# An S4D convolution with a token MLP: magnitude products moved into the openings of the sets, and the results of rows and columns taken out of PSUM behind the second half of E

## The chip, the cores and the metric

The kernel runs on one core of a Trainium2 chip. The metric is the device time of one execution in microseconds; lower is better.

## The reference, cut to what matters

```python
x = A_u                                                   # (1, 2048, 448)
mod = (silu(c) @ w_mod).reshape(..., 6, 1, -1)            # sa, ca, ga, sb, cb, gb
h = layernorm(x) * (1 + ca) + sa
# S4D: K[d, l] = 2 Re sum_n C[d, n] dt[d] exp((-exp(log_A_real) + i A_imag)[d, n] dt[d] l)
#      y = irfft(rfft(h, 4096) * rfft(K, 4096))[:2048] + h * D_skip        (d: 448, n: 256, l: 2048)
x = x + ga * S4D(h)
h = layernorm(x) * (1 + cb) + sb
x = x + gb * (gelu(h^T @ w1 + b1) @ w2 + b2)^T            # a token MLP, 2048 -> 1792 -> 2048
```

## The kernel before, in words

All of it is float32. The first half of the time makes the S4D convolution, the second half is the token MLP, which the change does not touch. The convolution is a Fourier transform in two stages. The transform of u (the normalised input) is made in **rows** (`u_rows`: 32 of them, each one matmul of 448 columns into PSUM and one VectorE instruction, L595, that adds the mean and multiplies by `mod`; two rows, a *pair*, share a tile `yt` of [128, 2, 448], and a pair's second row issues the DMA of the tile to `yu_d` in DRAM, L597) and then in **columns** (`u_cols`: 16 of them, each 8 matmuls of 448 columns into two PSUM tiles and two VectorE instructions, L631, and a DMA to `us_d`). Row pair p reads `xt[:, p]` and nothing else of `xt`.

The kernel K is generated in 56 *halves* s (16 channels of a group at a time). A half has these parts:

- **exponents and magnitudes** (`st_exponents`, `st_exp`): two Exp on ScalarE (L696) into `mag`;
- **phase** (`st_phase`, L667): eight matmuls on TensorE into the PSUM tiles `xe` and `xg`, of which there are two sets, so the phase of half s+1 writes where the E products of half s-1 have read;
- **sines** (`st_step`): six ScalarE instructions (L729 to L735);
- **G**: two products on GpSimd (L737, L738);
- **m2**, the magnitude product (`st_mag2`): a small product `w` (L712) and a large one (L717, `m`) on GpSimd;
- **E**: four products on VectorE, a first half E1 (L739, L740) that reads xe, and a second half E0 (L742, L743) that reads xg; two of the four read m2;
- **kgen** (`st_kgen`, L764): 64 small matmuls of E and G into `kg`, two halves later.

Every eighth half begins a *set*. `window(s)` first runs Exp for all eight halves of the set, e = 0 to 7 (Exp and Sin need different tables on ScalarE), and puts other work beside it; then the eight *steps* follow, one `st_step` each. Below, "window 8" is the opening of the set of halves 8 to 15, and "step 8" its first step. Ahead of the change the window computes m2 for the first two halves of its set (e < 2), and step s computes m2 of half s+2.

The instruction order of TensorE, ScalarE, VectorE and GpSimd is that of the code. What is not to run at once goes into lists of functions: `dve` for VectorE, `act` for ScalarE. `flush(dve)` is called by `between()`, which stands in `st_step` between E1 and E0; so the results of rows or columns whose matmuls stand behind step s are taken out of PSUM in step s+1, between its E1 and its E0. The rows and columns, `st_s1` (the next stage of K, L802) and the modulation share one pool of three PSUM tiles, `pms`. When `st_s1` has work in a step, `free` is false and the step gets no rows or columns. From half 8 on the order of SyncE, which issues nearly all DMAs, is a scheduler's.

`chain(q)` prepares the parameters of a group of 128 channels in small VectorE instructions, and `split` (L404, L406) cuts each result into two parts on GpSimd (`hl`, two buffers) and stores it to DRAM (`pars`). It runs mostly in the windows: `more(n)` makes n of its steps. Tile `xa` has one buffer; in window 16 ScalarE writes it for q = 3 (L451) when GpSimd's split of the old one is done. Set 32 and later run otherwise (`late_window`), and the change leaves them.

Pool `gp_` has three buffers of E, [128, 2, 16, 64]. Row pairs 2, 3 and 4 borrow E buffers (`yE`) for their `yt`; the other pairs share three buffers of `yt`. `m2p` has three buffers of m2. Weights of the modulation are loaded into `xt` (`wm_load`, L341, at steps 12 to 14 of the code): `xt[:, 0:4]`, then 4:8, then 8:12.

## Time and profile before

| | |
|---|---|
| runs | 663.27, 663.41, 668.56 us; median 663.41 us |
| profiled execution | 663.85 us, span 662.1 us, mean granted TensorE clock 0.984 |
| busy share of the span | PE 92%, DVE 67%, ACT 66%, POOL 41% |
| window 8 and its steps (us of the span) | about 64.7 to 82 and 82 to 114 |
| window 16 and its steps | about 114 to 133 and 133 to 163 |
| window 24 and its steps | about 163 to 178 and 178 to 206 |

PE is TensorE, DVE VectorE, ACT ScalarE, POOL GpSimd, SP SyncE; a row of the timeline gives the start, the duration and the instruction, and in brackets the idle time of its engine just ahead of it, with what ended it. Shares over the whole span mix the convolution with the MLP; the stretches in the table are where the changed code runs.

### The profile page before, as it was taken

Reading aid. Unit: us, or ns where it says so; the run is one execution under the profiler, and the core shown is the slowest. Engines: PE = TensorE matmul, PEld = TensorE weight load, DVE = VectorE, ACT = ScalarE, POOL = GpSimd, SP = SyncE. Lnnn points to the kernel's source line nnn. Section 1 sums busy time; section 2 is a strip of 40 time slices with the busy share of each in tenths; the row PEclk is TensorE's granted clock in tenths of the full one; section 3 lists DMA queues with packets and bytes.
Section 4 is the critical chain, followed back from the end, with each engine's and each line's share of the span. In section 5 each row is a group of like instructions: output and inputs, shape, how many; then the busy total and the mean of one; then the engine's idle time right before and its main releaser. Section 6 shows DMA issues by size and latency. Waiting matters only on the chain.

```text
span 662.1 us, 19161 instructions
## 1 busy us (share of the span) xinstructions
PE 612.3 (92%) x7639; PEld 442.9 (67%) x7639; DVE 443.0 (67%) x853; ACT 439.9 (66%) x828; POOL 269.5 (41%) x351
## 2 busy tenths in 40 slices
PE   1878998999999999999888999999999999999997
PEld 0444555445455565656544577788999999999996
DVE  8989889689894887868655688777422553333331
ACT  5978888899989999999587678885222522222220
POOL 7785597588599788787563000000000000000000
PEclk9998999989999999999999899999999999999999
DMA  6595747598775557576787999946755275555530
GB/s 145 156 219 166 253 143 257 182 248 268 218 247 178 103 166 218 169 215 182 234 274 227 257 247 234 233 112 196 201 160 153 57 209 164 162 160 166 161 106 28
DMA packets 97858, 123.67 MB, mean 187 GB/s; under 512 B 13717, under 2 KB 79801, under 8 KB 97769
## 3 DMA queue, kind: packets, MB, share of 16 engines
q1 hardware_dynamic: 97032, 120.02, 64.2%
q0 software_dynamic: 736, 2.43, 1.5%
q8 instruction: 60, 0.98, 0.7%
q14 instruction: 30, 0.24, 0.1%
HBM read 88.33 MB, written 33.59 MB: 184 GB/s over the span
## 4 chain that ended last, share of the span: by engine, by line
PE 63%; DMA 11%; DVE 9%; ACT 7%; POOL 4%; issue 4%; SPq 3%; ACTq 0%; DVEq 0%; POOLq 0%
PE o L1563 7%; PE o L1565 7%; PE o L1564 7%; PE acc L1400 6%; PE acc L1401 6%; PE acc L1402 6%; PE xe L667 6%; PE kg L764 6%; DMA w<-in_B_w_dram 3%; PE xg L667 3%; DMA xt<-in_A_u_dram 3%; DMA v_d<-vt 3%; PE pu L591 2%; PE vv L895 2%; PE kx L872 2%
## 5 line engine op out<-in xcount | busy, mean ns | idle before, releaser
L218 ACT CAST whi<-w 128x896 fp32r<-128x896 f32 x64 | 59.7, 939 | 138.5 <-PE o L1564 82.7
L227 DVE TENSOR_TENSOR wlo<-w,whi 128x896 fp32r<-128x896 f32 x64 | 68.1, 1086 | 41.4 <-ACT whi L218 35.1
L737 POOL TENSOR_TENSOR G<-mag,gs 128x512 f32<-128x512 f32 x56 | 71.9, 1283 | 36.4 <-ACT gs L733 36.4
L1400 PE MATMUL acc<-h3h,whi 128*128 128x448 f32 x224 | 83.0, 371 | 1.7 <-ACT h3h L1467 0.9
L1401 PE MATMUL acc<-h3l,whi 128*128 128x448 f32 x224 | 81.4, 363 | 0.5 <-DVE h3l L1474 0.3
L1563 PE MATMUL o<-uh,whi 128*128 128x448 f32 x224 | 81.3, 363 | 0.0
L1565 PE MATMUL o<-uh,wlo 128*128 128x448 f32 x224 | 81.2, 362 | 0.0
L1402 PE MATMUL acc<-h3h,wlo 128*128 128x448 f32 x224 | 81.0, 361 | 0.0
L1564 PE MATMUL o<-ul,whi 128*128 128x448 f32 x224 | 80.6, 360 | 0.0
L764 PEld LDWEIGHTS kg<-E,G 128*32 128x32 f32 x3584 | 56.2, 114 | 33.1 <-issue 18.4
L738 POOL TENSOR_TENSOR G<-mag,gs 128x512 f32<-128x512 f32 x56 | 71.9, 1285 | 0.0
L764 PE MATMUL kg<-E,G 128*32 128x64 f32 x3584 | 65.9, 227 | 6.4 <-issue 4.2
L667 PE MATMUL xg<-tab,lph 64*128 64x512 f32 x112 | 62.0, 553 | 6.6 <-DVE E L743 4.3
L1568 DVE TENSOR_TENSOR y<-o,x 128x448 f32<-128x448 f32 x16 | 10.0, 624 | 79.0 <-PE o L1565 79.0
L667 PE MATMUL xe<-tab,lph 64*128 64x512 f32 x112 | 61.9, 553 | 0.3 <-issue 0.2
L717 POOL TENSOR_TENSOR m<-mag,w 128x512 f32<-128x512 f32 x53 | 55.8, 1053 | 4.2
L1400 PEld LDWEIGHTS acc<-h3h,whi 128*128 128x128 f32 x224 | 42.0, 188 | 14.8 <-issue 2.1
L729 ACT ACTIVATE ab<-xe 128x512 f32<-128x512 f32 x56 | 33.9, 604 | 16.3 <-PE xg L667 9.1
L1401 PEld LDWEIGHTS acc<-h3l,whi 128*128 128x128 f32 x224 | 42.0, 187 | 3.8 <-DVE h3l L1474 0.9
L1565 PEld LDWEIGHTS o<-uh,wlo 128*128 128x128 f32 x224 | 42.1, 188 | 3.4
L1402 PEld LDWEIGHTS acc<-h3h,wlo 128*128 128x128 f32 x224 | 42.0, 187 | 3.1
L1564 PEld LDWEIGHTS o<-ul,whi 128*128 128x128 f32 x224 | 41.9, 187 | 3.0
(257 smaller groups left out, 1399.1 us busy)
## 6 DMA issues: line engine op xcount, KB each, us to landing
w<-in_B_w_dram SPq DMA_DIRECT2D x64, 224.0 KB
w<-in_B_w_dram SPq DMA_DIRECT2D x32, 448.0 KB
yi<-yu_d SPq DMA_DIRECT2D x32, 224.0 KB
us_d<-uo SPq DMA_DIRECT2D x16, 448.0 KB
u<-us_d SPq DMA_DIRECT2D x64, 112.0 KB
v_d<-vt SPq DMA_DIRECT2D x32, 224.0 KB
vt<-v_d SPq DMA_DIRECT2D x14, 448.0 KB
yu_d<-yt SPq DMA_DIRECT2D x13, 448.0 KB
```

Source lines behind the costliest of these rows:

```text
L218: self.nc.scalar.copy(hi, w)
L227: eng.tensor_tensor(lo, w, hi.bitcast(F32), ALU.subtract)
L667: T.matmul(out[k], lhs[r], rhs[r], start=start, stop=stop)
L737: G.tensor_tensor(Gt[:, 1], mg_, v32(sg), ALU.mult)
L738: G.tensor_tensor(Gt[:, 0], mg_, v32(cg_), ALU.mult)
L764: T.matmul(kg[32 * q : 32 * q + 32, m], Gt[:, c, d], E[:, c, d], start=h == 0 and c == 0 and m == 0, stop=h == 1 and c == 1, skip_group_ch ...
L1400: nc.tensor.matmul(acc[f], hi[:, fs], h3h[:, r], start=r == 0, stop=False)
L1401: nc.tensor.matmul(acc[f], hi[:, fs], h3l[:, r], start=False, stop=False)
L1402: nc.tensor.matmul(acc[f], lo[:, fs], h3h[:, r], start=False, stop=r == 15)
L1563: nc.tensor.matmul(o, hi[:, ks], uh[kh][:, k], start=kh == 0 and k == 0, stop=False)
L1564: nc.tensor.matmul(o, hi[:, ks], ul[kh][:, k], start=False, stop=False)
L1565: nc.tensor.matmul(o, lo[:, ks], uh[kh][:, k], start=False, stop=kh == 1 and k == 6)
```

## The change: what it does

1. **m2 in the sets.** Windows 8, 16 and 24 compute m2 for the first 4, 5 and 5 halves (`MSET`), where they computed it for 2; the steps compute 4, 3 and 3 where they computed 6 each. For the first two halves of a set m2 goes into an E buffer (`mE`) that the window takes.
2. **Rows by pairs.** Steps 8 to 14 make two rows each (14), where steps 9 to 14 made two or three (15); window 16 makes one more. No row pair borrows an E buffer any more: pairs 3, 4, 6, 8 and 14 use parts of `xt` that have been read (`spare`).
3. **Results at once.** In the steps of sets 8, 16 and 24 the results of rows and columns are taken out of PSUM at the end of the same step, behind E0 (`at_once`), not between E1 and E0 of the next. `more(pace[s])` moves to the end of the step too; where it stood it made no instruction in these sets.

```diff
-        yts, wurs, lent = {}, {}, []
+        yts, wurs = {}, {}
+        spare = {3: 0, 4: 1, 6: 2, 8: 3, 14: 6}
...
-                if pair in (2, 4):
-                    E = gp_.tile([P, 2, GD, NJ], F32, tag="E", name="yE")
...
-                yts[R, gp] = lent[pair - 2] if 2 <= pair < 5 else xp.tile([P, 2, D], F32, tag="yt", name="yt", bufs=3)
+                if pair in spare:
+                    yts[R, gp] = xt[:, 2 * spare[pair] : 2 * spare[pair] + 2]
+                else:
+                    yts[R, gp] = xp.tile([P, 2, D], F32, tag="yt", name="yt", bufs=3)
...
-            if s in (3, 4, 5):
+            if s in rooms:
+                m2 = rooms.pop(s)
+            elif s in (3, 4, 5):
...
+        def at_once(f, it, n):
+            k = len(dve)
+            some(f, it, n)
+            for out in dve[k:]:
+                out()
+            del dve[k:]
...
+            if s in (8, 16, 24):
+                E = gp_.tile([P, 2, GD, NJ], F32, tag="E", name="mE")
+                for k in range(2):
+                    rooms[s + k] = E[:, k].rearrange("p g j -> p (g j)")[:, 0:512].rearrange("p (d i) -> p d i", i=32)
...
-                elif s and (e < 2 or s >= 32):
+                elif s and e < (BATCH if s >= 32 else MSET[s // BATCH]):
                     st_mag2(s + e)
...
+        MSET = [0, 4, 5, 5]
...
-                if s < len(pace):
+                if s < len(pace) and not 8 <= s < 32:
                     more(pace[s])
...
+            if s == 8:
+                at_once(u_rows, rows, 2)
...
-            if s + 2 < 32 and (s + 2) % BATCH > 1 and s + 2 > 5:
+            if s + 2 < 32 and (s + 2) % BATCH >= max(2, MSET[s // BATCH]) and s + 2 > 5:
                 st_mag2(s + 2)
...
-            if 8 <= s < 16 and free:
-                some(u_rows, rows, 2 if s % 2 else 3)
+            if 8 < s < 16 and free:
+                at_once(u_rows, rows, 2)
...
             if 17 <= s < 32 and free:
-                some(u_cols, cols, 1)
+                at_once(u_cols, cols, 1)
+            if 8 <= s < 32 and s % BATCH != BATCH - 1:
+                more(pace[s])
```

VectorE in steps 10 and 11, before (E1 is L739 and L740, E0 is L742 and L743; `yt<-pu` are results of rows):

```order
L739 TENSOR_TENSOR E<-m_1359,xe 128x16x32
L740 SCALAR_TENSOR_TENSOR E<-mag,xe 128x16x32
L595 SCALAR_TENSOR_TENSOR yt<-pu,means,mod_105 128x448 x2
L742 TENSOR_TENSOR E<-mag,xg 128x16x32
L743 TENSOR_TENSOR E<-m_1359,xg 128x16x32
L739 TENSOR_TENSOR E<-m_1402,xe 128x16x32
L740 SCALAR_TENSOR_TENSOR E<-mag,xe 128x16x32
L595 SCALAR_TENSOR_TENSOR yt<-pu,means,mod_105 128x448 x3
L742 TENSOR_TENSOR E<-mag,xg 128x16x32
L743 TENSOR_TENSOR E<-m_1402,xg 128x16x32
```

The same place of the changed kernel (its lines are two further down; `xt<-pu` is a pair that uses a part of `xt`):

```order
L741 TENSOR_TENSOR E<-m_1140,xe 128x16x32
L742 SCALAR_TENSOR_TENSOR E<-mag,xe 128x16x32
L744 TENSOR_TENSOR E<-mag,xg 128x16x32
L745 TENSOR_TENSOR E<-m_1140,xg 128x16x32
L595 SCALAR_TENSOR_TENSOR xt<-pu,means,mod_105 128x448 x2
L741 TENSOR_TENSOR E<-m_1170,xe 128x16x32
L742 SCALAR_TENSOR_TENSOR E<-mag,xe 128x16x32
L744 TENSOR_TENSOR E<-mag,xg 128x16x32
L745 TENSOR_TENSOR E<-m_1170,xg 128x16x32
L595 SCALAR_TENSOR_TENSOR yt<-pu,means,mod_105 128x448 x2
```

The results have moved from between E1 and E0 to behind E0, ahead of the next step's E1, and there are two to a step.

GpSimd in window 16, before (`hl` are the chain's splits, `ks` a small sum for `st_s1`):

```order
L404 CAST hl<-ph 128x256
L784 TENSOR_TENSOR ks<-ks,dsk 128x8
L406 TENSOR_TENSOR hl<-ph,hl 128x256
L404 CAST hl<-p_1199 128x256
L406 TENSOR_TENSOR hl<-p_1199,hl 128x256
L404 CAST hl<-xa 128x256
L406 TENSOR_TENSOR hl<-xa,hl 128x256
```

And in the changed kernel:

```order
L404 CAST hl<-ph 128x256
L712 TENSOR_TENSOR w<-mag 128x16
L719 TENSOR_TENSOR m_2047<-mag,w 128x512
L786 TENSOR_TENSOR ks<-ks,dsk 128x8
L406 TENSOR_TENSOR hl<-ph,hl 128x256
L404 CAST hl<-p_1206 128x256
L712 TENSOR_TENSOR w<-mag 128x16
L719 TENSOR_TENSOR m_2075<-mag,w 128x512
L406 TENSOR_TENSOR hl<-p_1206,hl 128x256
L712 TENSOR_TENSOR w<-mag 128x16
L719 TENSOR_TENSOR m_2094<-mag,w 128x512
L404 CAST hl<-xa 128x256
```

Three pairs `w`, `m` stand ahead of the last split (`hl<-xa`) that stood behind step 16 to 18's G before.

SyncE in the steps of set 8, changed kernel (`yu_d<-xt` stores a pair out of `xt`, `yu_d<-yt` one out of a `yt` buffer; `xt<-in_w_mod_dram` are weights):

```order
L597 DMA yu_d<-xt 128x896
L341 DMA xt<-in_w_mod_dram 112x4x448
L597 DMA yu_d<-yt 128x896
L653 DMA lph_139<-pars_58 32x256
L657 DMA lph_139<-pars_58 64x1x256
L597 DMA yu_d<-yt 128x896
L341 DMA xt<-in_w_mod_dram 112x4x448
```

The first row is pair 8's store; the weights behind it overwrite the part of `xt` that it reads, so they now wait for that store to land, and pair 9's store stands behind them. Before, the weights waited there for matmuls alone.

More of the change, by code (lines that the diff above doesn't have):

```diff
@@ L581, in u_rows @@
                 pair = n // 2
-                if pair in (2, 4):
-                    E = gp_.tile([P, 2, GD, NJ], F32, tag="E", name="yE")
-                    rooms = E.rearrange("p a g j -> p (a g j)")[:, 0 : 4 * D].rearrange("p (h g d) -> p h g d", h=2, g=2)
-                    lent.extend(rooms[:, h] for h in range(2))
-                yts[R, gp] = lent[pair - 2] if 2 <= pair < 5 else xp.tile([P, 2, D], F32, tag="yt", name="yt", bufs=3)
+                if pair in spare:
+                    yts[R, gp] = xt[:, 2 * spare[pair] : 2 * spare[pair] + 2]
+                else:
+                    yts[R, gp] = xp.tile([P, 2, D], F32, tag="yt", name="yt", bufs=3)
             if g == 0 and R < 6:
@@ L639, in u_cols @@
                 u_load(p + 4)
-        mags, m2s, eg, phs = {}, {}, {}, {}
+        mags, m2s, eg, phs, rooms = {}, {}, {}, {}, {}
         v32 = lambda t: t.rearrange("p (d i) -> p d i", i=32)
```

## The prediction

> **What bounds the kernel now.** The page says where the whole time goes: TensorE is busy for 92%, and most of its chain is the MLP, which the change leaves. So I read the three stretches that it touches, each from the first sine of a set to the last.
>
> Busy time of each engine by stretch (us, instructions in brackets):
>
> ```profile
> core 0: us, PE busy (x) PEld busy (x) DVE busy (x) ACT busy (x) POOL busy (x), PEclk, DMA share, GB/s
> 78.90:111.30 32.40, 30.06 (x562) 17.02 (x558) 28.82 (x50) 27.61 (x53) 27.57 (x31) 1.00 0.69 218
> 130.90:160.30 29.40, 28.14 (x515) 14.83 (x516) 26.53 (x47) 27.00 (x54) 25.30 (x28) 0.94 0.92 252
> 174.30:204.40 30.10, 27.95 (x608) 15.58 (x610) 27.80 (x47) 27.11 (x52) 27.06 (x32) 1.00 0.73 232
> ```
>
> No engine has much room: DVE, ACT and POOL are each busy for 86 to 92% there. A step must be looked at singly. Steps 27 and 28 on POOL, then on DVE, then on PE (timeline, start and duration):
>
> ```profile
> 189.74 1.28 POOL L737 TENSOR_TENSOR G<-mag,gs 128x512 f32<-128x512 f32 x1
> ...
> 192.22 0.25 POOL L712 TENSOR_TENSOR w<-mag 128x16 f32<-128x16 f32 x1
> 192.54 1.05 POOL L717 TENSOR_TENSOR m<-mag,w 128x512 f32<-128x512 f32 x1
> 193.55 1.27 POOL L737 TENSOR_TENSOR G<-mag,gs 128x512 f32<-128x512 f32 x1
> ...
> 192.06 0.68 DVE L739 TENSOR_TENSOR E<-m,xe 128x512 f32<-128x512 f32 x1
> ...
> 193.26 1.26 DVE L631 SCALAR_TENSOR_TENSOR uo<-mod,svt,pu 128x448 f32<-128x448 f32 x2
> 194.44 0.68 DVE L742 TENSOR_TENSOR E<-mag,xg 128x512 f32<-128x512 f32 x1
> ...
> 195.64 0.68 DVE L739 TENSOR_TENSOR E<-m,xe 128x512 f32<-128x512 f32 x1
> ...
> 191.31 1.10 PE L764 MATMUL kg<-E,G 128*32 128x64 f32 x64
> ...
> 193.45 1.51 PE L627 MATMUL pu<-yi,s 64*64 64x448 f32 x8
> ```
>
> POOL has no gap and a period of 193.55 - 189.74 = 3.81 us, of which `w` and `m` take 193.55 - 192.22 = 1.33. DVE has none either, with a period of 195.64 - 192.06 = 3.58: four E products at 0.60 and two results (`uo`) at 0.59 from start to start. On PE 193.45 - 191.31 = 2.14 hold kgen (1.03) and the phase (1.1); the columns' matmuls behind them (`pu`) take 1.51, since they wait for a PSUM tile that DVE empties. POOL is the slower one and yet does not set the pace, since kgen needs G two halves later. It does once in the set, in its last step, on ACT:
>
> ```profile
> 202.49 0.60 ACT L733 ACTIVATE gs<-xg 128x512 f32<-128x512 f32 x1 [0.52 <-POOL G L737]
> ```
>
> So in the middle of a set **DVE is the bound**, and POOL's lag is paid once, at 0.52 us. Where else DVE waits is the next question; steps 9 to 15 on DVE:
>
> ```profile
> 85.58 0.69 DVE L739 TENSOR_TENSOR E<-m,xe 128x512 f32<-128x512 f32 x1 [0.58 <-ACT xe L732]
> 89.63 0.69 DVE L739 TENSOR_TENSOR E<-m,xe 128x512 f32<-128x512 f32 x1 [1.24 <-POOL w L712]
> ...
> 104.32 1.27 DVE L595 SCALAR_TENSOR_TENSOR yt<-pu,means,mod 128x448 f32<-128x448 f32 x2 [1.50 <-DMA yu_d<-yt]
> ...
> 114.44 1.28 DVE L808 COPY yk<-y 128x512 f32<-128x512 f32 x2
> ```
>
> and where POOL and DVE begin the set:
>
> ```profile
> 82.54 1.29 POOL L737 TENSOR_TENSOR G<-mag,gs 128x512 f32<-128x512 f32 x1 [5.55 <-ACT gs L733]
> 82.54 0.68 DVE L739 TENSOR_TENSOR E<-m,xe 128x512 f32<-128x512 f32 x1
> ```
>
> **The change, part by part.**
>
> *Set 8: -2.9 us.* E of half 8 starts at 82.54, and the copies behind E of half 15 start at 114.44: 31.9 us. In them lie 32 E products at 0.60 (19.1) and 15 results at 0.595 (8.9), so 28.0 of work and 3.9 of waiting. Afterwards there are 14 results (8.3), so 27.4 of work. Of the waits, 0.58 goes, since the two results of step 8 now fill it. The 1.50 goes as well: it is a store that had not landed when its `yt` buffer was wanted again, and with `spare` the buffers are wanted later (the pair that waits is three pairs after its buffer's last user, and pairs 8 and 14 no longer take one). The 1.24 is named for POOL, but `w` cannot hold E1; ACT was late:
>
> ```profile
> 87.92 0.64 ACT L729 ACTIVATE ab<-xe 128x512 f32<-128x512 f32 x1
> 83.81 1.16 PE L802 MATMUL y<-wc,ks 64*64 64x64 f32 x64
> 84.90 1.26 PE L679 MATMUL kg<-ones 128*128 128x256 bf16 x10
> ```
>
> A new wait takes its place. `y` needs two of the three PSUM tiles of `pms`; with the two rows of step 8 ahead of it on PE, one of its tiles is free only when DVE has taken out the first result, at about 84.9 + 0.6 = 85.5 instead of 83.8. Behind `y` on PE's queue stand the ten warming matmuls and the phase of half 10, so that phase ends at about 85.5 + 1.1 + 1.2 + 1.1 = 88.9, ACT starts half 10 there and not at 87.92, and DVE waits about 1.0 for the rows of step 9, which stand behind that phase. I keep 1.2 of waiting in all: 82.5 + 27.4 + 1.2 = 111.1 and about 0.2 of loose ends, so 111.3 against 114.4 on DVE; ACT's last sine comes about 2.9 earlier. From both ends: 0 (the waits come back elsewhere) to -4.5 (all 3.9 go, and a result).
>
> *Window 8: +0.15.* POOL makes two more pairs `w`, `m` there, 2.7 us; its wait of 5.55 ahead of the first G (above) covers them. But one pair stands ahead of `ks`, which `y` needs:
>
> ```profile
> 73.67 0.21 POOL L784 TENSOR_TENSOR ks<-ks,dsk 128x8 f32<-128x8 f32 x1
> 75.03 1.52 PE L802 MATMUL y<-wc,ks 64*64 64x64 f32 x64
> ```
>
> `ks` ends 1.33 later, at 75.2, and PE takes `y` at 75.03 now. Bounds 0 and 1.33.
>
> *Window 16: +1.4.* Three pairs more, 3 x 1.32 = 3.96, in the middle of the chain's splits. POOL waits there as follows:
>
> ```profile
> 124.06 0.40 POOL L404 CAST hl<-ph 128x256 fp32r<-128x256 f32 x1 [1.22 <-DVE ph L419]
> 125.73 0.40 POOL L404 CAST hl<-p 128x256 fp32r<-128x256 f32 x1 [0.35 <-DVE p L425]
> 129.19 0.40 POOL L404 CAST hl<-xa 128x256 fp32r<-128x256 f32 x1 [2.25 <-DVE xa L445]
> 129.66 0.72 POOL L406 TENSOR_TENSOR hl<-xa,hl 128x256 fp32r<-128x256 f32 x1
> 130.53 0.35 ACT L451 ACTIVATE xa<-A_C_real 128x128 f32<-128x128 f32 x1
> ```
>
> The pairs stand behind the first of these splits, so the idle 0.35 and 2.25 behind them cover 2.60; the remaining 3.96 - 2.60 = 1.36 makes `hl<-xa` end at 131.7 instead of 130.38. L451 on ACT overwrites `xa`, started at 130.53, 0.15 after that end, and has all sines of half 16 behind it on ACT's queue. So what is off the path in POOL's idle time sits on the path at this one place: the set starts 1.2 to 1.4 later, and I take 1.4. Lower end 0. Upper end: DVE's own products with two SBUF operands may be held by POOL's; the same instruction took
>
> ```profile
> 62.13 0.43 DVE L434 TENSOR_TENSOR xa<-xa,A_C_real 128x256 f32<-128x256 f32 x1
> 126.31 0.91 DVE L434 TENSOR_TENSOR xa<-xa,A_C_real 128x256 f32<-128x256 f32 x1
> ```
>
> with POOL idle and with POOL in a split. Three such holds of 0.48 give +1.4 more, so +2.8 for the upper end. The Trainium skill's page "SBUF — State Buffer", section "Who interferes with whom", has a rule for it that speaks against this change: a DVE instruction with two SBUF inputs and a GpSimd one that reads SBUF exclude each other, and the second to come is blocked until the first ends. [...] By the rule each moved `m` could hold a DVE product for its whole 1.05; three of them would make this window 3.2 worse, and the sum +0.5 in place of -2.65.
>
> *Set 16: -0.8.* Here the columns' results now run where DVE waited for ACT.
>
> ```profile
> 137.96 2.17 PE L627 MATMUL pu<-yi,s 64*64 64x448 f32 x8
> 143.14 0.98 PE L627 MATMUL pu<-yi,s 64*64 64x448 f32 x8
> 143.30 0.60 ACT L729 ACTIVATE ab<-xe 128x512 f32<-128x512 f32 x1 [1.27 <-PE xg L667]
> 144.97 0.69 DVE L739 TENSOR_TENSOR E<-m,xe 128x512 f32<-128x512 f32 x1 [0.69 <-POOL w L712]
> 147.36 0.68 DVE L742 TENSOR_TENSOR E<-mag,xg 128x512 f32<-128x512 f32 x1
> ```
>
> The first columns take PE 2.17 us where the next take 0.98 (their data come late), phase 19 follows late, ACT waits, and E1 of half 19 starts at 144.97. Then the results of step 18 went ahead of E0 (147.36). Now they stand ahead of E1, in DVE's waiting time: matmuls done at 143.14 + 0.98 = 144.1, results to 145.3, E1 to 146.5, E0 from 146.5: 0.8 earlier. From there DVE has no gap, before or after, and the gain keeps its size. Bounds 0 and -1.5 (all of DVE's waits in the set's first four steps).
>
> *Set 24: -0.5.* DVE runs without a gap through the first six steps, and E0 of each half ends where it did, since the same results come ahead of it; E1 comes later, which nobody waits for. PE no longer waits for a PSUM tile (1.51 above for columns that take 0.98), but DVE was the bound. What is left is ACT's 0.52 for POOL, which goes, as POOL has three pairs less. In window 24 the three pairs again stand among splits; the last split ends perhaps 0.9 later and so does G of half 24, but kgen of that half stands two steps later, and G of the next halves catches up without its `m`, so I cost it at nothing; if that cover went it would be 0.9.
>
> The eight pairs taken off POOL in the steps, 8 x 1.33 = 10.6, are therefore worth only the 0.5. Sets 32 to 48 keep their code and move as a block.
>
> **Sum:** -2.9 + 0.15 + 1.4 - 0.8 - 0.5 = -2.65, against the profiled execution's 663.85: 661.2. That execution was 0.44 above the median of the runs (663.41), to which the new runs will be compared, so I predict **660.8**, or 0.4% less. About 1% is what can be told from no change here.
>
> **Rivals.**
>
> *POOL is the bound after all* (the change does what its words suggest): every pair saved shortens its step, 663.4 - 10.6 = 652.8. For it: POOL without a gap in all three sets. Against it: DVE without a gap at 3.58 beside POOL's 3.81, and a single wait of ACT for G. Chance 0.03.
>
> *The splits hide the moved pairs:* window 16 costs nothing, since the 0.15 of slack is larger than shown or DVE is earlier; 660.8 - 1.4 - 0.15 = 659.2. For it: POOL is busy for half of each window. Against: the 1.36 above. Chance 0.20.
>
> *SyncE gives set 8's gain back.* The loads of `w_mod` into `xt` now wait in SyncE's order for pair stores to land, with pair 9's store behind; step 14's results want that buffer.
>
> ```profile
> 96.50 7.72 DMA yu_d<-yt
> ```
>
> In the chain of waits a store lands 7.72 us after its issue. Pair 8's results end at about 94.5 and its store lands between 98 and 102 (half of 7.72, and all of it); then pair 9's store takes until 102 to 110. By my count the buffer is wanted at 107.7. At the late end DVE waits 2.3 there and the stores behind add to it, so set 8's 2.9 is gone: 663.7. For it: the DMA share of 0.69 in that stretch. Against: only the ends together are late. Chance 0.15.
>
> *POOL's moved products hold DVE's.* The hold of 0.48 shown above meets the chain's products in windows 16 and 24 six times: 2.9, so 663.7. For it: those two rows. Against: DVE has waits of its own in the windows that would take part of it. The page named above would have each hold last up to 1.05, which makes 6.3 and 667.1. Chance 0.08.
>
> *The results stand in DVE's way* (the other side). `at_once` puts DVE behind matmuls of the same step at 18 places, with the next E1 queued behind the result. From the end of the last E0, PE needs 1.1 for the phase and 0.98 for the columns, DVE gets there after 3.58: slack 1.5. It decides when PE runs more than 1.5 late in each step, as where columns took 2.17 for 0.98 (+1.19) and kgen 1.86 for 1.03 (+0.83):
>
> ```profile
> 140.13 1.86 PE kg L764 x64
> ```
>
> Together 2.02, so 0.5 a step and 9 us over 18 steps without set 16's and 24's gains (1.3): 660.8 + 9 + 1.3 = 671; in half of the steps 666.6. Against it: in the steady part PE has 1.03 + 1.1 + 0.98 = 3.1 of work for 3.58. Chance 0.08, half of that over 1% slower.
>
> **How the numbers follow.** Forecast 0.46 (its own range 659.7 to 662.4, each term within half of its bounds), rivals 0.03, 0.20, 0.15, 0.08 and 0.08. The range from 658.4 (hidden pairs, and all of set 16's waits) to 664.4 (either of the two at 663.7, and window 24's 0.9) leaves out the first and the last rival and some tail. Faster by over 1%: the first rival and a tail of the second, 0.04. Slower by over 1%: 0.04. Within: 0.92.
>
> **What would show it.** Right: DVE from E of half 8 to the copies behind half 15 in about 29 us; L451 in window 16 waiting for POOL's L406 by over 1 us; no ACT wait for G in step 31; POOL with gaps in the sets, without gain from them. Wrong: DVE waits ahead of L595 or L631 for PE in most steps; a DMA wait at step 14; a period below 3.5 us in the middle of a set.

## The result and the profile after

| | before | after |
|---|---|---|
| median of 12 runs each, in turn | 664.22 us (662.07 to 669.44) | 668.85 us (666.13 to 672.97) |
| ratio, 95% interval | | 1.0072 [1.0048, 1.0096] |
| span of the profiled execution, mean granted clock | 662.1 us, 0.984 | 665.5 us, 0.982 |

The changed kernel is 0.7% slower; 660.8 us was forecast, within 658.4 to 664.4. The page's first block, after:

```profile
span 665.5 us, 19164 instructions
PE 609.0 (92%) x7639; PEld 444.0 (67%) x7639; DVE 447.9 (67%) x853; ACT 440.5 (66%) x828; POOL 270.9 (41%) x351
```

Each engine has as many instructions as before, but DVE is busy for 4.9 us more (443.0 before): single DVE instructions have become longer. The loss is read by stage. In the table a window runs from its first Exp (L696) to the second E1 product of its first half (L742 after, L740 before); set 8 runs from there to the last sine of half 15 (L737, L735 before), and set 16 or 24 to the first Exp of the next window. The last column is the start of half 33's first E0 product (L744, L742 before), and behind it all kernels have the same instructions. The labels are those of the experiments below.

| us | window 8 | set 8 | window 16 | set 16 | window 24 | set 24 | half 33 at |
|---|---|---|---|---|---|---|---|
| before | 18.43 | 27.66 | 18.50 | 29.90 | 15.05 | 26.17 | 221.77 |
| after | 19.22 | 28.33 | 20.92 | 28.82 | 16.12 | 25.55 | 225.40 |
| e1_products_only | 21.18 | 27.06 | 19.49 | 30.59 | 15.61 | 25.78 | 225.16 |
| e2_rows_only | 18.67 | 27.22 | 17.54 | 29.88 | 15.21 | 25.78 | 220.71 |
| e3_step8_behind | 19.55 | 28.81 | 20.87 | 28.95 | 16.44 | 25.55 | 226.49 |
| e4_windows_8_only | 20.03 | 26.98 | 17.54 | 29.90 | 15.33 | 25.77 | 221.73 |
| e5_no_rows_in_8 | 20.31 | 25.71 | 24.13 | 29.40 | 16.26 | 25.55 | 227.10 |
| e6_late_pairs | 19.82 | 27.99 | 19.68 | 28.48 | 15.15 | 27.56 | 224.28 |
| e7_memsets | 18.66 | 27.21 | 20.32 | 29.86 | 16.01 | 25.81 | 224.23 |
| e8_products_twice | 19.18 | 26.98 | 19.96 | 29.84 | 15.54 | 26.07 | 224.11 |
| e10_rows_only_9_10 | 19.59 | 26.40 | 18.37 | 29.89 | 14.61 | 26.45 | 220.99 |
| e11_window_8_rows_9_10 | 20.27 | 25.72 | 18.75 | 29.87 | 14.55 | 27.03 | 221.68 |
| e12_third_pair_early | 18.95 | 26.70 | 18.14 | 29.53 | 15.76 | 25.56 | 221.33 |
| e13_rows_9_10_again | 19.33 | 25.69 | 24.37 | 29.15 | 15.91 | 25.56 | 226.71 |
| e14_windows_16_24 | 19.00 | 26.65 | 19.95 | 30.01 | 16.42 | 25.57 | 223.70 |

How far profiles differ without a change of the code is seen in stretches with the same instructions: window 8 with two pairs takes 18.43 to 19.59, and the stretch from half 33 to the end 440.1 to 444.4. A single cell is good to about 1 us; below, the table is used where several rows agree, and the timed ratios for the rest. (The profile of e9_rows_9_10 was taken in a disturbed execution and isn't used; e13_rows_9_10_again is the same kernel.)

**Window 16.** DVE in the changed kernel:

```profile
126.02 0.85 DVE L423 TENSOR_SCALAR u<-ph 128x256 f32<-128x256 f32 x1
126.91 0.99 DVE L425 TENSOR_TENSOR p<-ph,u 128x256 f32<-128x256 f32 x1
...
128.88 1.14 DVE L436 TENSOR_SCALAR A_C_imag<-A_C_imag 128x256 f32<-128x256 f32 x1
130.05 0.84 DVE L438 SCALAR_TENSOR_TENSOR xa<-xa,A_C_imag 128x256 f32<-128x256 f32 x1
...
131.39 1.02 DVE L443 TENSOR_SCALAR u<-xa 128x256 f32<-128x256 f32 x1
132.44 0.43 DVE L445 TENSOR_TENSOR xa<-xa,u 128x256 f32<-128x256 f32 x1
```

POOL at the same time, and ACT behind it:

```profile
125.67 1.05 POOL L719 TENSOR_TENSOR m<-mag,w 128x512 f32<-128x512 f32 x1
...
126.89 0.72 POOL L406 TENSOR_TENSOR hl<-ph,hl 128x256 fp32r<-128x256 f32 x1
128.69 1.18 POOL L719 TENSOR_TENSOR m<-mag,w 128x512 f32<-128x512 f32 x1
129.84 0.77 POOL L406 TENSOR_TENSOR hl<-p,hl 128x256 fp32r<-128x256 f32 x1
131.07 1.19 POOL L719 TENSOR_TENSOR m<-mag,w 128x512 f32<-128x512 f32 x1
132.94 0.40 POOL L404 CAST hl<-xa 128x256 fp32r<-128x256 f32 x1 [0.68 <-DVE xa L445]
...
134.17 0.31 ACT L451 ACTIVATE xa<-A_C_real 128x128 f32<-128x128 f32 x1 [2.33 <-POOL hl L406]
```

The three moved products end at 126.72, 129.87 and 132.26; L423, L436 and L443 of DVE end at 126.87, 130.02 and 132.41, each 0.15 behind one of them. L425 and L438 end in the same way, 0.3 behind the two L406. The stretch from L423's start to L445's end takes 132.87 - 126.02 = 6.85 us. The same on DVE in e2_rows_only, which has two products in this window, as before:

```profile
123.83 0.36 DVE L423 TENSOR_SCALAR u<-ph 128x256 f32<-128x256 f32 x1
124.23 0.43 DVE L425 TENSOR_TENSOR p<-ph,u 128x256 f32<-128x256 f32 x1
...
126.13 0.28 DVE L436 TENSOR_SCALAR A_C_imag<-A_C_imag 128x256 f32<-128x256 f32 x1
126.45 0.43 DVE L438 SCALAR_TENSOR_TENSOR xa<-xa,A_C_imag 128x256 f32<-128x256 f32 x1
...
127.36 0.29 DVE L443 TENSOR_SCALAR u<-xa 128x256 f32<-128x256 f32 x1
127.69 0.43 DVE L445 TENSOR_TENSOR xa<-xa,u 128x256 f32<-128x256 f32 x1
```

It takes 128.12 - 123.83 = 4.29. So of the 3.4 us by which window 16 is longer than in e2_rows_only, 2.56 are held DVE instructions, not a delay in POOL's queue: POOL waits for DVE (0.68 ahead of `hl<-xa`), and not the other way. This does not vary from profile to profile: the stretch takes 6.84 to 6.95 in all seven with the three products among the splits (the changed kernel, e1, e3, e5, e8, e13, e14), 4.28 or 4.29 in the six without (e2, e4, e6, e10, e11, e12), and 4.6 before.

**Set 8.** The waits went and came back. DVE, PE and ACT in the set, after:

```profile
86.81 1.28 DVE L595 SCALAR_TENSOR_TENSOR xt<-pu,means,mod 128x448 f32<-128x448 f32 x2 [1.27 <-PE pu L591]
91.80 1.27 DVE L595 SCALAR_TENSOR_TENSOR yt<-pu,means,mod 128x448 f32<-128x448 f32 x2 [1.33 <-PE pu L591]
87.55 1.15 PE L804 MATMUL y<-wc,ks 64*64 64x64 f32 x62 [0.52 <-DVE xt L595]
85.62 0.60 ACT L731 ACTIVATE ab<-xe 128x512 f32<-128x512 f32 x1 [2.12 <-PE xg L667]
91.10 0.60 ACT L731 ACTIVATE ab<-xe 128x512 f32<-128x512 f32 x1 [1.29 <-PE xg L667]
102.79 0.60 ACT L735 ACTIVATE gs<-xg 128x512 f32<-128x512 f32 x1 [0.27 <-POOL G L739]
107.17 0.60 ACT L735 ACTIVATE gs<-xg 128x512 f32<-128x512 f32 x1 [1.01 <-POOL G L739]
110.98 0.60 ACT L735 ACTIVATE gs<-xg 128x512 f32<-128x512 f32 x1 [0.59 <-POOL G L739]
```

ACT, which starts the next window 5.3 us behind its last sine, waits 3.4 us for phases at the set's start and then 1.87 for POOL's G. On DVE the set is 1.1 shorter (from E of half 8 at 83.07 to the copies at 113.84; it was 31.9 long), on ACT 0.7 longer.

### The profile page after: what moved, and what is told of

Its sections match the earlier page's. It is cut to its first block, busy times and chain, and to the rows that moved or that the text cites. A ratio compares the mean times of both kernels' runs of the same rounds, so it can differ in the third digit from the quotient of the medians.

```text
span 665.5 us, 19164 instructions
## 1 busy us (share of the span) xinstructions
PE 609.0 (92%) x7639; PEld 444.0 (67%) x7639; DVE 447.9 (67%) x853; ACT 440.5 (66%) x828; POOL 270.9 (41%) x351
## 4 chain that ended last, share of the span: by engine, by line
PE 69%; ACT 9%; DVE 6%; DMA 6%; issue 4%; POOL 3%; SPq 1%; ACTq 0%; POOLq 0%; DVEq 0%
PE xe L667 8%; PE o L1585 7%; PE o L1584 7%; PE o L1583 7%; PE kg L766 6%; PE acc L1420 6%; PE acc L1421 6%; PE acc L1422 6%; PE xg L667 4%; DMA w<-in_B_w_dram 3%; PE vv L897 2%; PE kx L874 2%; PE y L804 2%; PE pu L591 2%; PE pu L627 2%
## 5 line engine op out<-in xcount | busy, mean ns | idle before, releaser
L739 POOL TENSOR_TENSOR G<-mag,gs 128x512 f32<-128x512 f32 x56 | 71.9, 1285 | 44.8 <-ACT gs L735 44.7
L740 POOL TENSOR_TENSOR G<-mag,gs 128x512 f32<-128x512 f32 x56 | 71.9, 1284 | 0.0
L667 PE MATMUL xg<-tab,lph 64*128 64x512 f32 x112 | 63.9, 570 | 6.4 <-ACT gs L736 3.0
L667 PE MATMUL xe<-tab,lph 64*128 64x512 f32 x112 | 63.6, 568 | 3.8 <-ACT gs L736 2.7
L719 POOL TENSOR_TENSOR m<-mag,w 128x512 f32<-128x512 f32 x47 | 49.9, 1061 | 3.7
L731 ACT ACTIVATE ab<-xe 128x512 f32<-128x512 f32 x56 | 33.8, 604 | 15.7 <-PE xg L667 8.8
L1583 PEld LDWEIGHTS o<-uh,whi 128*128 128x128 f32 x224 | 41.9, 187 | 3.0
```

What stands on the lines that cost most here:

```text
L667: T.matmul(out[k], lhs[r], rhs[r], start=start, stop=stop)
L739: G.tensor_tensor(Gt[:, 1], mg_, v32(sg), ALU.mult)
L740: G.tensor_tensor(Gt[:, 0], mg_, v32(cg_), ALU.mult)
L1583: nc.tensor.matmul(o, hi[:, ks], uh[kh][:, k], start=kh == 0 and k == 0, stop=False)
```

## The experiments

**e1_products_only**: the kernel before with part 1 of the change (`MSET`, `mE`, the condition in the steps). 

> The kernel before with one part of the change alone: the eight more pairs of products in the windows (two in window 8, three each in windows 16 and 24), rows and columns as before. Theory A: these pairs cost what the changed kernel loses in its three windows (0.8, 2.3 and 1.1 us between the landmarks of the two traces, 4.2 in all, less about 0.5 for the lighter sets), because POOL's products hold DVE's instructions of the chain and stand ahead of the splits: about 3.7 us over the kernel before, ratio 1.0055. Rival B: the pairs are free in the windows and the loss comes from the rows' and columns' results standing elsewhere: ratio 1.000 or below.

Measured: 669.67 us, ratio 1.0064 [1.0036, 1.0093]. The products alone cost what the whole change costs. By stage it came otherwise than theory A had it: window 8 is 2.75 longer than before (L457, L459 and L461 on DVE are held, 3.00 us together for 1.66), and window 16 only 1.0; the stretch from L423 to L445 is as long there as in the changed kernel, but begins 7.2 us behind the window's first Exp, where it began at 8.4 before (the granted clock over 108 to 124 us is 1.00 in e1 and 0.89 before).

**e2_rows_only**

```diff
-        MSET = [0, 4, 5, 5]
+        MSET = [0, 2, 2, 2]
-            if s in (8, 16, 24):
-                E = gp_.tile([P, 2, GD, NJ], F32, tag="E", name="mE")
-                ...
```

> The changed kernel with two products in each window as before (and without the E buffer lent to them); rows by pairs and the results right behind E's second half stay. Theory A: the windows give back 4.2 us, the sets lose some 0.5 to 1.5 to POOL, which has the products in its steps again: 665 to 666, ratio to before 1.001 to 1.003. Rival B: the time stays within 0.5 us of the changed kernel's 668.9, ratio 1.007.

Measured: 664.90, ratio 0.9997 [0.9973, 1.0022]; half 33 starts 1.06 earlier than before in the profile. So rows by pairs and the earlier results are worth about nothing, at most 0.3%, and not 2.9 + 0.8. Why is on POOL in set 8, whose first G, second idle time and last G of the set are:

```profile
83.41 1.28 POOL L739 TENSOR_TENSOR G<-mag,gs 128x512 f32<-128x512 f32 x1 [6.48 <-ACT gs L735]
92.03 1.28 POOL L739 TENSOR_TENSOR G<-mag,gs 128x512 f32<-128x512 f32 x1 [0.41 <-ACT gs L735]
112.30 1.26 POOL L740 TENSOR_TENSOR G<-mag,gs 128x512 f32<-128x512 f32 x1
```

POOL works for 30 us and waits 0.41 once. ACT waits for it (`gs` has three buffers), 2.15 us in its last sines. With DVE relieved and the products in the steps, **POOL bounds set 8** (e10, below, tests it).

**e3_step8_behind**: the two rows of step 8 behind `st_s1`, and so behind `y`.

```diff
-            if s == 8:
-                at_once(u_rows, rows, 2)
             held = s > 32 and s % BATCH == BATCH - 2
             free = s > 7 and not st_s1(...)
+            if s == 8:
+                at_once(u_rows, rows, 2)
```

> The changed kernel with the two rows of step 8 behind the first inverse product of the kernel columns (y) instead of ahead of it. Theory A1: set 8 lost its gain because these rows hold a PSUM tile that y waits for, with the warming matmuls and phase 10 behind it on PE: phase 10 about 1.5 us earlier and the end 1 to 2 us earlier than the changed kernel, 667.3. Rival A2: set 8's second half is bound by POOL, which starts late and then runs without a gap to the set's end: the set ends where it did unless POOL starts earlier too, 668.9.

Measured: 673.91, ratio 1.0119 [1.0080, 1.0158]: worse, a miss for both. The second row now waits for y's tile, which ACT empties behind all of its sines, and half 10's phase stands behind it. PE, then ACT:

```profile
88.31 1.02 PE L591 MATMUL pu<-xt,wur 64*128 64x448 f32 x2 [1.71 <-ACT yk L810]
91.73 0.60 ACT L731 ACTIVATE ab<-xe 128x512 f32<-128x512 f32 x1 [2.98 <-PE xg L667]
```

Three PSUM tiles don't hold two rows and y; the order only says who waits. The profile explains 1.1 us over the changed kernel (half 33 at 226.49); it is of the fastest of the six runs (668.63), and where the other runs lose their 5 us isn't shown.

**e4_windows_8_only**: `MSET = [0, 4, 2, 2]`. 

> The changed kernel with the additional products in window 8 alone (4, 2 and 2 pairs in the three windows). Theory A: windows 16 and 24 give back 2.3 and 1.1 us, and sets 16 and 24 lose at most 0.6 of that: about 666.0, ratio to before 1.003; and the chain's instructions on DVE in window 16 are back at 0.28 to 0.43 us each except beside the splits. Rival B: 668.9.

Measured: 667.89, ratio 1.0037 [1.0013, 1.0061]. The profile shows windows 16 and 24 as in e2_rows_only (17.54 and 15.33) and half 33 0.04 earlier than before; the timed runs say 0.4% slower. Between those two lies the stretch behind half 33: 444.4 us here and 443.9 in e11, which has the same `MSET`, but 440.1 to 443.2 in the others. Part of it looks alike in these two: kgen and the matmuls behind it, right at half 33, take 1.71 and 1.76 (1.80 and 1.76 in e11), where they take 1.10 and 0.98 in e10. So it may belong to the kernel, and window 8's cost is open between 1 and 3 us (e11, below, against e10 leaves the same gap: 0.7 by half 33, 2.3 by the medians).

**e5_no_rows_in_8**: no rows in step 8, three in steps 11 and 13. 

> The changed kernel without rows in step 8; steps 11 and 13 make three rows instead. Theory A: rows and y in one step share three PSUM tiles, so that whichever comes second waits, and the phase of half 10 behind it; without them the last sine of half 10 comes 3.95 us behind that of half 9, as in the kernel before, and not 5.48; POOL, which ran without a gap from there on, starts earlier too, and the set ends 1.1 to 1.5 us earlier than in the changed kernel: about 667.6. Rival B: POOL's own sum bounds the set wherever the phase stands, or the three rows cost as much: 668.9.

Measured: 670.08, ratio 1.0100 [1.0056, 1.0145]. The first half of theory A holds: half 10's last sine comes 3.95 behind half 9's (5.48 in the changed kernel), and set 8 ends 2.6 sooner on ACT (25.71). Then DVE waits 2.79 for a store at step 14, and all is lost in window 16 (24.13), so that the time is over rival B's 668.9 as well.

**e6_late_pairs**: the additional pairs behind the last split of each window.

```diff
-                elif s and e < (BATCH if s >= 32 else MSET[s // BATCH]):
+                elif s and e < (BATCH if s >= 32 else 2):
                     st_mag2(s + e)
...
+            if 0 < s < 32:
+                for e in range(2, MSET[s // BATCH]):
+                    st_mag2(s + e)
             aside.clear()
```

> The changed kernel with the additional pairs of products behind the last split of each window instead of among the splits (two, three and three, as before). Theory A: what they cost is the holding of DVE's instructions of the chain by POOL's products; behind the chain there is nothing to hold, and POOL sits idle 2.4 to 4.0 us ahead of the first G of each set. Window 8 gives back 0.8 us, window 16 2.6 and window 24 1.0, less up to 1 for a G that comes late: 665 to 666. Rival B: POOL's time in the window is what costs: the first G comes later by what is moved, 668 to 669.

Measured: 668.74, ratio 1.0061 [1.0034, 1.0089]: rival B's time, and nothing is gained. ACT does begin half 16 (L731) 14.1 us behind the window's first Exp, as against 17.3 in the changed kernel and 13.9 in e2_rows_only. But the next piece of the chain now meets POOL's products (m, then the first G). POOL, then DVE ahead of E of half 16:

```profile
131.86 1.05 POOL L719 TENSOR_TENSOR m<-mag,w 128x512 f32<-128x512 f32 x1
...
134.34 1.31 POOL L739 TENSOR_TENSOR G<-mag,gs 128x512 f32<-128x512 f32 x1
131.93 1.07 DVE L461 TENSOR_SCALAR s<-s 128x128 f32<-128x128 f32 x1
...
134.56 1.24 DVE L470 SCALAR_TENSOR_TENSOR s<-t,s 128x128 f32<-128x128 f32 x1
135.72 0.68 DVE L741 TENSOR_TENSOR E<-mE,xe 128x512 f32<-128x512 f32 x1
```

In the changed kernel, where the products lie earlier, L461 and L470 take 0.22 and 0.29; here they end 0.09 and 0.15 behind m and G. The hold goes where the products go.

**e7_memsets** and **e8_products_twice**: e2_rows_only with three POOL instructions of 1.3 us (or pairs) more in windows 16 and 24, whose result nobody reads.

```diff
                     st_mag2(s + e)
+                if s in (16, 24) and e in (2, 3, 4):
+                    G.memset(fill.rearrange("p a g j -> p (a g j)")[:, 0:1400], 0.0)
```

In e8 the added lines are those of `st_mag2`, with `fill` for m2. 

> The kernel with rows by pairs and two products per window (e2_rows_only), with three memsets of about 1.3 us on POOL in windows 16 and 24, where the changed kernel has its three additional pairs; they write a buffer that nobody reads. Theory A: DVE is held by POOL instructions that read two SBUF operands; memsets read none, so the chain's instructions from L423 to L445 in window 16 take 4.3 us as without them, and the time rises only by a late split, 0 to 1.2 us over e2_rows_only's 664.9. Rival B: any occupation of POOL costs the same, by its queue or its port: 6.8 us for that stretch, and about 668.

> The kernel with rows by pairs and two products per window (e2_rows_only), with the products of halves 18 to 20 and 26 to 28 computed once more, into a buffer that nobody reads, at the places in windows 16 and 24 where the changed kernel has its additional pairs; the steps keep theirs. Theory A: the windows cost what they do in the changed kernel, 3.4 us for window 16 and 1.0 for window 24, without the relief of 1.1 to 1.4 us in the sets: 664.9 + 4.4 = 669.3; the stretch from L423 to L445 takes 6.8 us. Rival B: the products cost nothing in the windows and it was their absence from the steps that moved other work: 665.

Measured: e7 669.63, ratio 1.0094 [1.0060, 1.0129]; e8 667.94, ratio 1.0068 [1.0045, 1.0092]. Memsets cost as much as products: theory A of e7 falls. POOL and DVE in window 16 of e7:

```profile
122.55 1.27 POOL L1163 MEMSET fill<- 128x1400 f32 x1
125.39 1.26 POOL L1163 MEMSET fill<- 128x1400 f32 x1
127.32 1.27 POOL L1163 MEMSET fill<- 128x1400 f32 x1
123.26 0.71 DVE L423 TENSOR_SCALAR u<-ph 128x256 f32<-128x256 f32 x1
125.12 1.69 DVE L432 TENSOR_SCALAR A_C_real<-A_C_real 128x256 f32<-128x256 f32 x1
127.59 1.15 DVE L436 TENSOR_SCALAR A_C_imag<-A_C_imag 128x256 f32<-128x256 f32 x1
```

The memsets end at 123.82, 126.65 and 128.59, the three TENSOR_SCALAR at 123.97, 126.81 and 128.74: 0.15 behind each, as with the products. L432 takes 0.48 elsewhere. The stretch from L423 to L445 is 130.45 - 123.26 = 7.19 us. The results out of PSUM (L595) keep their length beside a memset. So a DVE TENSOR_SCALAR from SBUF to SBUF is held by POOL whether POOL reads SBUF or only writes it. The Trainium skill's page "SBUF — State Buffer", section "Who interferes with whom", has it so: copies, casts and tensor_scalar can run in a two-port mode that takes the port pair shared with GpSimd, and the second to come waits for all of the first; two SBUF inputs collide with a GpSimd instruction that reads. The trace agrees with the first by L436, which began 0.27 behind a memset and took 1.15 for 0.28. (L432 began 0.27 ahead of one, but 0.06 behind a CAST of POOL, and was held through both.) For the second no DVE instruction with two SBUF inputs began beside a memset here; L425, beside L406, which reads, was held (0.98 for 0.43).

e8 tells that the products' cost in the windows does not come from the steps they leave: with the steps unchanged half 33 starts 3.4 later than in e2_rows_only, of which window 16 has 2.4. The stretch from L423 to L445 takes 6.85, as theory A has it; the time is 1.4 below theory A's 669.3.

**e9_rows_9_10** and, once more for its profile, **e13_rows_9_10_again**:

```diff
-            if s == 8:
-                at_once(u_rows, rows, 2)
...
             if 8 < s < 16 and free:
-                at_once(u_rows, rows, 2)
+                at_once(u_rows, rows, 3 if s < 11 else 2)
```

> The changed kernel without rows in step 8; steps 9 and 10 make three rows instead (in e5_no_rows_in_8 it was 11 and 13, which put pair 9's store one step later, and step 14's results waited 2.79 us for it). Theory A: both waits of set 8 are gone, the one of half 10's phase and the one for the store; from E1 of half 8 to the last sine of half 15 it is 25.7 us, against 28.3 in the changed kernel and 27.7 before, and window 16 starts 2 us earlier than in the changed kernel: 666.8. Rival B: step 14 still waits over 1 us for the store, since the whole set runs ahead of it: 668 or more.

> e9_rows_9_10 once more, for a profile that can be read by stage. Theory A: set 8 (E1 of half 8 to the last sine of half 15) takes 25.7 us as in e11_window_8_rows_9_10, whose set 8 has the same instructions, and step 14 waits at most 0.2 us for the store; what is lost lies in windows 8, 16 and 24 (0.8, 2.4 to 3.4 and 1.0), and the time is 1 to 2 us below the changed kernel's. Rival B: window 16 takes back what set 8 gains, since its held chain on DVE and not ACT's start sets the end of that window: time as in the changed kernel, and window 16 over 21 us from its first exponential to E1 of half 16.

Measured: 669.77, ratio 1.0065 [1.0039, 1.0090], and 669.66, ratio 1.0059 [1.0035, 1.0084]. Set 8 takes 25.69 on ACT, as theory A has it, and yet the time stays, and window 16 takes 24.37. That is the outcome of both rivals B, but the cause seen is the one that e9's names, the store: step 14 waits 3.48 for it. DVE and PE at the set's end, e13:

```profile
111.77 1.27 DVE L595 SCALAR_TENSOR_TENSOR yt<-pu,means,mod 128x448 f32<-128x448 f32 x2 [3.48 <-DMA yu_d<-yt]
112.50 1.98 PE L804 MATMUL y<-wc,ks 64*64 64x64 f32 x62 [2.11 <-DVE yt L595]
115.34 1.28 DVE L810 COPY yk<-y 128x512 f32<-128x512 f32 x2
```

SyncE's queue shows why (L597 stores rows, L341 loads weights of the modulation, here into `xt[:, 4:8]`), and so does its list of waits (us in all, times, the longest):

```profile
99.21 0.40 SPq L597 DMA_DIRECT2D yu_d<-xt  x1
105.10 0.34 SPq L341 DMA_DIRECT2D xt<-in_w_mod_dram  x1
105.54 0.44 SPq L597 DMA_DIRECT2D yu_d<-yt  x1
```

```profile
SPq L341 <- DMA yu_d<-xt: 6.5, 2, 5.4
```

From 99.61 to 105.10 SyncE waits to overwrite a part of `xt` (pair 8's, by `spare`) whose store, issued at 99.21, must land first. Pair 9's store stands behind it and is issued at 105.54; step 14 wants pair 9's `yt` back. In e10 and e11 this load is issued at 101.22 and 102.06, and step 14 waits 0.3. Why SyncE is 2 to 3 us later in e5 and e13 than in e11, whose set 8 has the same instructions as e13's, is open. The granted clock of TensorE (the number ahead of the last two) is lowest in e13 too; e13, then the changed kernel, then e2:

```profile
115.00:125.00 10.00, 9.63 (x153) 5.40 (x153) 5.86 (x11) 5.00 (x12) 4.98 (x8) 0.67 0.53 205
115.00:125.00 10.00, 10.00 (x156) 5.88 (x148) 4.89 (x12) 7.68 (x15) 4.77 (x9) 0.72 0.40 147
115.00:125.00 10.00, 9.73 (x131) 4.79 (x124) 6.41 (x15) 8.44 (x18) 6.28 (x12) 0.91 0.46 163
```

The ten microseconds cut a slow time that lies earlier in e2: over 108 to 124 us the mean is 0.68, 0.79 and 0.79, so that e2 and the changed kernel do not differ there.

**e10_rows_only_9_10**, **e11_window_8_rows_9_10** and **e12_third_pair_early** look for a version that beats both: rows as in e9, with `MSET` [0, 2, 2, 2], [0, 4, 2, 2] and [0, 2, 3, 3], the last with its third pair ahead of `more`:

```diff
+                if s in (16, 24) and e == 2:
+                    st_mag2(s + 2)
                 if s < 32:
                     more(WPACE[s // 8][e])
```

> e2_rows_only (rows by pairs, results behind E0, two products in each window) without rows in step 8, three rows in steps 9 and 10. Theory A: with the products in the steps POOL bounds set 8 (30.1 us of work, idle for 0.4), so the wait of half 10's phase costs nothing and its removal gives 0 to 0.4: 664.7. Rival B: the waits of PE and ACT at step 10 bound the set: 1.5 us earlier, 663.4.

> Products 4, 2 and 2 in the windows and rows by pairs with none in step 8 and three in steps 9 and 10. Theory A: POOL has two pairs less in set 8 and no wait takes that up: E1 of half 8 to the last sine of half 15 in 25.7 us, 1.5 less than in e2_rows_only; window 8 costs 0.9 to 1.1 for DVE's held instruction; 664.4 in all, or as the kernel before and a little less. Rival B: window 8 costs as much as set 8 gains, or the store is late at step 14: 665.5 or more.

> Products 2, 3 and 3 in the windows, the third pair of windows 16 and 24 ahead of the split of ph, where POOL sits idle (1.3 us in e2_rows_only) and DVE waits for PE or takes results out of PSUM; rows as in e10_rows_only_9_10. Theory A: POOL's products hold only DVE instructions that read and write SBUF alone, so this pair costs nothing there, and sets 16 and 24, which POOL bounds with its products in the steps, give 0.4 and 0.1: 664.2, the fastest so far. Rival B: the split of ph comes later by the pair's 1.3 us and all behind it: 665.5.

Measured, with the ratio to before: e10 664.92, 1.0004 [0.9985, 1.0022]; e11 667.18, 1.0030 [1.0011, 1.0049]; e12 664.14, 0.9992 [0.9968, 1.0015]. None beats the kernel before. In e10 set 8 is 0.8 shorter on ACT than in e2, more than theory A gave and less than rival B. The 0.8 are POOL's: it works for 29.75 us from the first G to the last without a gap (0.41 in e2), and its first G begins 0.41 sooner behind E of half 8 (0.06 for 0.47). So POOL bounds the set here as well; the time of the kernel is the same. In e11 it takes 25.72, as expected, and window 8 takes it back (20.27), with 667.18 over both expectations' bounds: rival B. e12 agrees with theory A in time (664.2 expected) but can't be told from e10; only its set 16 (29.53, against 29.84 to 29.90 with two pairs) hints at the relief. Its third pair does hold a TENSOR_SCALAR (L417, 1.02 for 0.29), against theory A's reason, but window 16 is no longer for it (18.14, 18.37 in e10).

**e14_windows_16_24**: e9 with `MSET = [0, 2, 5, 5]`. 

> The changed kernel with products 2, 5 and 5 in the windows (the additional pairs in windows 16 and 24 alone) and the rows as in e9_rows_9_10. Theory A: against e10_rows_only_9_10 (664.9) windows 16 and 24 cost 2.4 and 0.6 to 1.0, and sets 16 and 24 give back 1.1 and 0.4: 666.4 to 666.8. Rival B: the sets give back nothing, 668, as with the products computed twice.

Measured: 667.57, ratio 1.0059 [1.0035, 1.0083], nearer to rival B: window 16 costs 1.6 us against e10, window 24 1.8, set 16 gives back nothing (30.01) and set 24 0.9. The ratios of [4, 2, 2] (e11, 1.0030) and [2, 5, 5] (1.0059) both lie above 1. By their middle values windows 16 and 24 have the larger part of the loss, but the intervals overlap.

## Why the prediction was wrong, point by point

| term | predicted | measured, after less before | what it was |
|---|---|---|---|
| set 8 | -2.9 | +0.7 on ACT (-1.1 on DVE) | failed step |
| window 8 | +0.15 | +0.8 | too small |
| window 16 | +1.4 (0 to 2.8) | +2.4 (+3.4 against e2) | failed step: DVE held, not POOL late |
| set 16 | -0.8 | -1.1 | size right, reason wrong |
| window 24 | 0, or 0.9 | +1.1 | the cover went |
| set 24 | -0.5 | -0.6 | right in size |

The rest of the 3.6 us by which half 33 is late is window 32 (+0.7, same instructions) less a start that came 0.26 earlier. Set 8 came out 3.6 us worse than forecast and the three windows 2.7 together; either alone would have left the sum within the range or at its end (664.4, 663.5), both did not. Two sums of the prediction are off by 0.2, without weight: set 8's on DVE gives 114.4 - 111.3 = 3.1 and not 2.9, and 663.7 with window 24's 0.9 gives 664.6 and not 664.4.

*Set 8 is the step that failed first, in three ways.* "So in the middle of a set DVE is the bound" was read from a kernel in which DVE and POOL had nearly the same pace, 3.58 and 3.81. The lag was taken to be paid once; but a rhythm 0.23 slower shows as soon as DVE no longer waits, and e2 shows POOL without a gap and ACT waiting for it. The rival "POOL is the bound after all" had 0.03; for set 8 it was right once DVE was relieved, though not for the whole time it gave. Second, "ACT's last sine comes about 2.9 earlier" carried a gain of DVE over to ACT. The next window's first Exp comes 5.3 us behind that sine in every kernel, and e2 gains 2.3 between the second E1 product of half 8 and E0 of half 15 on DVE (27.85 for 30.12), but only 0.4 on ACT. Whether DVE's lead is worth something in the window is open: e2 and e4 have 17.54 for window 16 and before has 18.50, but e10 to e12 have 18.1 to 18.8, and no timed run shows a gain. Third, the new wait for a PSUM tile was named rightly, rows and y in step 8 and half 10's phase behind them, but priced at 1.2 for all where half 10 alone came 1.5 later (5.48 for 3.95). Half 9 came another 1.1 late, and not by that wait: its phase stands behind a wait of PE for the last rows of window 8, 1.67 for 1.16 before, and ran at a lower clock, its first matmuls taking 0.79, where half 10's take 0.50:

```profile
81.09 1.02 PE L591 MATMUL pu<-xt,wur 64*128 64x448 f32 x2 [1.67 <-DVE xt L595]
83.43 0.79 PE L667 MATMUL xe<-tab,lph 64*128 64x512 f32 x1
```

That wait is for results (L595) that stand on DVE behind L461, which is held in window 8 (below). It makes half 9 late by itself: in e3, without the slow phase, half 9's last sine comes 4.72 behind half 8's, 3.59 before and 5.21 in the changed kernel. The slow phase adds to it; of the other profiles only e1 has one, and in e13 PE waited 2.07 there and the same matmuls took 0.50, so what brings it about is not shown.

The rival "SyncE gives set 8's gain back" (0.15) had the mechanism to the line: in the changed kernel step 14 waits only 0.16, since the set is late anyway, but where experiments took the first waits out it came, 2.79 and 3.48, above the 2.3 that was priced.

*Window 8, 16 and 24: the hold.* Window 16 is the second step that failed. The prediction's 1.4 was a split that comes late in POOL's queue; POOL waited 0.68 for DVE ahead of that split, and what came late was DVE's chain. Holds stood in the term's upper end and in a rival, for products with two SBUF operands alone. The Trainium skill's page "SBUF — State Buffer", section "Who interferes with whom", exempts DVE instructions with one SBUF input only outside the two-port modes, and by the trace the chain's TENSOR_SCALAR are not exempt. In window 8 (POOL, then DVE)

```profile
76.66 1.19 POOL L719 TENSOR_TENSOR m<-mag,w 128x512 f32<-128x512 f32 x1
76.86 1.14 DVE L461 TENSOR_SCALAR s<-s 128x256 f32<-128x256 f32 x1
```

L461 took 0.28 before, and RECIPROCAL, L595 and E stand behind it. (L459 ahead of it was held before, 0.72, and is not now, 0.42, so 0.5 of window 8's 0.8 is the hold's.) In window 24 L434 took 1.02 for 0.30. The hold was priced at 0.48, the one that showed, where it lasts to the end of the POOL instruction: up to 0.86 each beside m in the changed kernel. The rival "POOL's moved products hold DVE's" (0.08) was the mechanism, but in part for other instructions than it names, and without set 8's loss; that its price by the page, 667.1, was the nearest number in the prediction is in part luck. Of window 16's 3.4 over e2, 2.6 are holds. The rest lies ahead of them: L423 begins 8.8 us behind the window's first Exp, 7.8 in e2, and kgen ahead of it took 1.75 for 1.10, since the slow time of the clock reaches into it here. In e8 and e14 L423 begins at 7.8 as well, and the window is 2.4 longer than in e2, which is the holds alone. In window 24 G of half 24 came late as the prediction allowed, and TensorE's phase ahead of it (ACT waits 1.43 for it).

*Set 16.* The results taken out earlier give nothing alone (e2: 29.88 for 29.90), nor do the products moved alone (e1: 30.59); with both it is 28.5 to 29.4 in five of six profiles, and 30.01 in e14. That it takes both agrees with two engines of like pace; why e14 has no gain is not settled.

*What was right:* "no ACT wait for G in step 31"; POOL's gaps in sets 16 and 24 without much gain; a period of 3.58 in the sets' middle; ACT's L451 waiting over 1 us for L406 (2.33). The rival on the other side, results in DVE's way, did not show: DVE waits for the rows' matmuls in steps 8 and 9 alone, and for no columns in the steps of sets 16 and 24.

## What to carry to other kernels

Work moved into an engine's idle time is not free if it holds the engine that is on the path there: look at what the neighbour runs at that moment, and price the hold by the whole length of the moved instruction. Where two engines have nearly the same pace, taking work off one shows the other at once; count both, and follow the gain to the engine that starts the next stage. A new wait hides the next one behind it (a PSUM tile, then a store in SyncE's order), so that a term of several removed waits is worth little until the last of them is gone.

## What the runs showed of the hardware

A VectorE TENSOR_SCALAR in float32 from SBUF to SBUF was held by GpSimd's product and by its memset alike, until 0.15 us behind the end of either (0.28 became 1.14 beside the product and 1.15 beside the memset), and so were instructions with two SBUF inputs beside a reading one (0.43 became 0.99). RECIPROCAL beside a GpSimd product (L1140, window 8) kept its 1.75, and L595, with an operand in PSUM, its 0.68 beside a memset (e7). GpSimd's own became longer too (`w` 0.42 for 0.25, `m` 1.19 for 1.05). The granted clock of TensorE fell to 0.50 for some microseconds around the start of window 16 in most profiles; over 108 to 124 us its mean was 0.68 in e5 and e13, where TensorE had waited longest ahead of `y` (2.6 and 3.3 us), but with the same wait of 1.7 it was 0.79 in e2 and the changed kernel and 0.89 in e4 and e8. No run shows what brings it about.
